# A fused attention and MLP kernel: the masks as second transfer, new planner constants and ranks

## The chip, the cores and the metric

The kernel runs on one core of a Trainium2 chip. A core has five engines that run their own instruction streams, each in order: TensorE (PE, matrix products; its weight loads are shown apart as PEld), VectorE (DVE), ScalarE (ACT), GpSimd (POOL) and SyncE (SP), which here issues all transfers between the chip's memory (HBM) and the on-chip memory (SBUF). Products accumulate in a small second on-chip memory, PSUM. The metric is the time of one execution on the device in microseconds (us), as the median of several runs.

## What is computed

Attention with two kinds of local masks, followed by a two-layer network whose activation is a rational function:

```python
scores = scale * np.matmul(q, k.transpose(0, 1, 3, 2))      # 8 batches, 8 heads, 576 x 64
mask_plain = (rel >= 0) & (rel < 32)                        # heads 0 to 3
mask_dil = (rel >= 0) & (rel < 128) & (rel % 4 == 0)        # heads 4 to 7
scores = np.where(masks[None, :, :, :], scores, -1000000000.0)
attn = softmax(scores)
x = (attn @ v), as 4608 tokens x 512
h = x @ w_in                                                # 512 -> 2048
P = a[0] + a[1] * h + a[2] * h**2 + a[3] * h**3
Q = 1.0 + np.abs(b[0]) * np.abs(h) + np.abs(b[1]) * h**2
out = (P / (Q + 1e-06)) @ w_out                             # 2048 -> 512
```

The two weight matrices come as 64-bit floats; the kernel takes their 32-bit words apart and joins them to 32-bit floats.

## The kernel before

**Attention in units.** Each of the 8 batches is cut into 6 units (48 in all, numbered batch * 6 + unit). A unit loads one tile of queries and keys (`load_qk`, 448 KB) and one of values (`load_v`, 384 KB). In the first two batches PE writes the masks into PSUM with a product by an identity and adds the scores to it (`scores`, lines 274 to 285), so a unit's scores need its qk and the masks `mask_t`, a 96 KB tile that is loaded once (line 903). Then follow the row maximum (`mx`, DVE), its subtraction, the exponential (ACT), the sum and reciprocal (DVE), the normalization (POOL), transposes (PE) with a copy (`pT`), and the product with the values (`av`). For the six units of batch 0 ACT evacuates the result to the high part of the MLP's input (`evac_hi`, tile `xh`) and DVE takes the low part (`xl`); each value is kept as a sum of two parts, for products at full precision. Batches from 2 on add the masks on DVE and turn their tiles by transposes on DVE and transfers.

**The MLP in tiles.** 9 chunks of 512 tokens times 16 slices of the hidden layer make 144 tiles, in an order given by `runs` and `tiles` (lines 963 and 964). A tile is 12 matmuls of PE into `h`, a chain on ACT, DVE and POOL (absolute value, the two linear parts, a logarithm and an exponential for the division, the products), and 12 matmuls `out` for four output banks. The first tiles need their slice of the weights: `plan_weights` (line 689) loads a 512 KB block (`wi0` to `wi15`, `wo0` to `wo15`), takes the words apart on ACT and POOL, joins them on DVE and splits the result in a high and a low part.

**The order is planned.** Nothing is issued directly. Each step is an `Op` with the engines that could run it, a cost in ns for each, a rank, its dependencies (`deps`), ops that must only be issued before it (`follows`) and buffers that it takes. `Plan.run` (line 128) simulates the engines at build time: again and again it takes the engine that can start first, picks the op of lowest rank among those that can start within 200 ns, and emits its instructions. What it emits is pinned, so each engine's instructions stand in the planner's order on the chip, and an instruction that waits holds back all that stand behind it on its engine. Transfers are planned as one pipe: the first is not through before `DMA_START`, each adds its bytes over `DMA_RATE`, and `DMA_NS` passes from the end of its bytes to its use (lines 86 and 170 to 172).

**Ranks.** The ranks are in units of one tile's number. `Plan.due` (line 106) counts backward: an op with a slack gets the least rank of what needs it, less its own cost over `PERIOD`, less its slack. A unit is due (`by`) at `last - (5 - u) * step`, with a pair (last, step) for each batch in `DUE` (line 32). Tiles from the 37th on get their steps' ranks from `LATE` (line 34), slacks come from `SLACK` (line 35): `qk0` and `v0` for the loads of batch 0, `wi`, `wo`, `w` and `out` for the weights and the early tiles. All loads of batch 0 and of the weights are sorted by rank, and each follows the one before it (lines 980 to 982).

The masks (`masked`, rank -39.4) and the six coefficients a and b (`lc`, rank -39.5, planned with 60 ns on SP) are two transfers more; the masks follow the coefficients. `coefs` (line 910, rank -30) prepares the coefficients with one small instruction on DVE and one on ACT; the first tile of the MLP needs it.

Of the kernel before, what the change touches and what calls it, by code (L numbers as in the profile page):

```python
# [28 lines left out]
START_S, START_O = ["A", "att"] * 3, ["B", "B", "B", "A", "B", "A"]  # L29
KIND = [0, 0, 0, 0, 1, 0] + [2] * 6  # L30
LESS = [0, 0, 0, 0, 1, 1]
DUE = [(-41.16, 11.47), (-146.25, 19.43), (423.68, 72.57), (61.95, 5.87), (470.95, -17.55), (494.47, -17.25), (93.76, -24.29), (711.56, 21.96)]

LATE = {"ab": -187.16, "ql": -342.11, "pl": -25.5, "qq": -118.36, "t1": -2.55, "t2": -120.77, "ln": 177.41, "ex": -496.7, "g0": -73.65, "g1": -54.63, "g2": -312.0, "gh": -189.38, "gl": 379.92, "out": 3.83}
SLACK = {"sc": 2.49, "qk0": -51.8, "v0": -50.12, "load": 7.26, "wi": 11.43, "wo": -2.45, "w": -16.22, "gl": -5.19, "out": -6.13}

EARLY_TILES, BOTH_TILES = 36, 36

# [40 lines left out]
class Plan:  # L79
# [3 lines left out]
    HOP = {"PE": 200.0, "ACT": 135.0, "DVE": 120.0, "POOL": 80.0, "SP": 0.0}  # L83
    MORE = {("PE", "ACT"): 40.0, ("ACT", "POOL"): 110.0, ("DVE", "POOL"): 110.0, ("DVE", "ACT"): 60.0, ("ACT", "DVE"): 15.0}
    DUE_HOP, WINDOW = 150.0, 200.0
    DMA_START, DMA_NS, DMA_RATE = 3300.0, 1750.0, 375.0
    PERIOD, PE_LATE = 4743.0, 105.0

    def __init__(self):
# [2 lines left out]
    def op(self, engs, rank, fn, *deps, dma=0, lock=False):  # L92
        o = Op(engs, rank, fn, deps, dma, lock)
        self.ops.append(o)
        return o
# [88 lines left out]
def tile_attention_moe(  # L184
# [21 lines left out]
    op = plan.op  # L206

    def load(dst, src):
        pin(nc.sync.dma_start(dst, src))  # L209
# [4 lines left out]
    def act(o, i, func, **kw):  # L214
        pin(nc.scalar.activation(o, i, func, **kw))  # L215

    def tt(o, x, y, op):
        pin(nc.vector.tensor_tensor(o, x, y, op))  # L218

    def stt(o, x, s, y, op0, op1):  # L220
        pin(nc.vector.scalar_tensor_tensor(o, x, s, y, op0, op1))  # L221
# [7 lines left out]
    def either(eng, o, x, y, alu):  # L229
        (ptt if eng == "POOL" else tt)(o, x, y, alu)  # L230
# [26 lines left out]
    class Unit:  # L257
# [251 lines left out]
        def plan(self, by, tags):  # L509
# [59 lines left out]
            for o in (sc, ma, mx, su, ex, sm, rc, no, tr, *self.placed, *([sb] if kind == 2 else [])):  # L569
                o.slack = 0.0  # L570
            sc.slack = SLACK["sc"]
            lq.slack = SLACK["qk0" if start else "load"]
            lv.slack = SLACK["v0" if start else "load"]
            plan.takes(lq, qt, 1 if start else LOADS, [sc])
# [67 lines left out]
    early, first_loads, unit_loads, left_done = [], [], [], []  # L642
# [46 lines left out]
    def plan_weights(key):  # L689
        f = op({"SP": 430}, 0, lambda e: w_fetch(key), dma=512 * (8 if wide else 4) * P)  # L690
        early.append(f)
        if len(joined) >= AHEAD:
            f.follows.append(joined[-AHEAD])
        if wide:
            sc = op({"ACT": 600}, 0, lambda e: w_scale(key), f)
            lw = op({"ACT": 690, "POOL": 690}, 0, lambda e: w_low(key, e), f, consts)
            jn = op({"DVE": 680}, 0, lambda e: w_join(key), sc, lw, lock=True)
            steps = [sc, lw, jn]
        else:
            steps = [op({"DVE": 335}, 0, lambda e: w_copy(key), f)]  # L700
        hi = op({"ACT": 550, "DVE": 460, "POOL": 620}, 0, lambda e: w_hi(key, e), steps[-1], lock=True)
        lo = op({"DVE": 602, "POOL": 1280}, 0, lambda e: w_lo(key, e), hi, lock=True)
        plan.takes(steps[0], "stage", STAGE, [lo])
        plan.takes(f, "%s%d" % key, 1, [steps[-1]])
        plan.takes(hi, "%s%d" % key, 1, [lo])
        joined.append(steps[-1])
        w_done[key] = lo
        for o in steps + [hi]:
            o.slack = 0.0
        lo.slack = SLACK[key[0]]  # L710
        f.slack = SLACK["w"]

# [10 lines left out]
    class Tile:  # L723
# [51 lines left out]
        def plan(self):  # L775
# [5 lines left out]
            Tile.last_h = h  # L781
            ab = op({"ACT": 480}, k + LATE["ab"], lambda e: self.abs(), h)
            ql = op({"ACT": 710}, k + LATE["ql"], lambda e: self.q_lin(), ab)
            pl = op({"ACT": 664}, k + LATE["pl"], lambda e: self.p_lin(), h)
            if tail:
                pl.follows.append(ql)
            qq = op(both, k + LATE["qq"], lambda e: either(e, self.a, self.r, self.a, ALU.mult), ql, lock=True)
            t1 = op({"DVE": 602}, k + LATE["t1"], lambda e: tt(self.t, self.t, self.ps, ALU.mult), pl, ab)
            t2 = op({"DVE": 663}, k + LATE["t2"], lambda e: stt(self.ps, self.t, na_t[:, 1:2], self.ps, ALU.add, ALU.mult), t1)
            ln = op({"ACT": 615}, k + LATE["ln"], lambda e: act(self.r, self.a, AF.Ln, bias=ln_bias, scale=2.0**-LOG_SHIFT), qq)  # L790
# [7 lines left out]
            if self.early:  # L798
                for o in (ab, ql, pl, qq, t1, t2, ln, ex, g0, g1, g2, gh):
                    o.slack = 0.0  # L800
                gl.slack = SLACK["gl"]
            outs = []
# [81 lines left out]
    coef_t = const.tile([P, 6], F32, name="coef_t")  # L884
# [3 lines left out]
    def make_coefs():  # L888
        pin(nc.vector.tensor_scalar(na_t, coef_t[:, 0:4], -1.0, None, ALU.mult))
        act(ab_t, coef_t[:, 4:6], AF.Abs)  # L890
# [7 lines left out]
    def memsets():  # L898
        pin(nc.gpsimd.memset(low_bias, LOW_BIAS))
        pin(nc.gpsimd.memset(ln_bias, GUARD * 2.0**-LOG_SHIFT))  # L900
        pin(nc.gpsimd.memset(exp_bias, -LOG_SHIFT * 0.6931471805599453))

    masked = op({"SP": 430}, -39.4, lambda e: load(mask_t, mask), dma=P * 768)
# [1 line left out]
    minus, less_ops = [], []  # L905
    plan.takes(identity, "gl", 2, less_ops)
    consts = op({"POOL": 80}, -87, lambda e: memsets())
    lc = op({"SP": 60}, -39.5, lambda e: load(coef_t, coef), dma=3000)
    masked.follows.append(lc)
    coefs = op({"DVE": 80}, -30, lambda e: make_coefs(), lc, consts)  # L910


# [1 line left out]
    for u in range(NU):  # L914
        tags = ((wpool, f"wi{15 - u}"), (wpool, f"wo{15 - u}"))
        last, step = DUE[0]
        Unit(0, u).plan(last - (NU - 1 - u) * step, tags)
    for key in keys:
        plan_weights(key)
    for b in range(1, B):  # L920
        last, step = DUE[b]
        for u in range(NU):
# [124 lines left out]
```

## Time and profile before

| | |
|---|---|
| median of 3 runs | 917.04 us (916.18 to 917.08) |
| the profiled execution | 916.49 us, of which the span from the first to the last instruction is 914.7 us |
| busy in the span | PE 883.2 us (97%), PEld 716.1, DVE 742.3 (81%), ACT 675.4 (74%), POOL 467.7 (51%) |
| instructions | 21129, of these 8153 matmuls |
| transfers | 103.46 MB, mean 113 GB/s |
| chain that ended last | PE 75%, DVE 11%, DMA 5%, ACT 5%, issue 3% |

The times in the profile run from the start of the span. A row of the timeline gives start, length, engine, line, operation, the written and the read tiles, and in brackets the idle time before it with what ended that. The row of a transfer on SPq is its issue; it lands later. The windows give busy times of each engine within a stretch, the granted clock of PE and the share and rate of the transfers. Where several instructions of one kind follow each other they are merged, with x and their count.

### The profile page before, as it was taken

The numbers are of one execution on the slowest core, as the hardware profiler recorded it, in microseconds if no ns is written. First come the engines' busy times: TensorE is split into PE (matmuls) and PEld (weight loads), VectorE is DVE, ScalarE is ACT, GpSimd is POOL, SyncE is SP. The second block draws the span as 40 slices with busy tenths as digits, with TensorE's granted clock in tenths as the row PEclk, the third lists the DMA queues.
The fourth block names the chain that finished last, engine by engine and source line by source line (L and its number), as shares of the span: only waits on it lengthen the run. The fifth ranks groups of instructions, "written<-read, shape, count | busy, mean of one in ns | idle before, by whom it ended". The sixth has DMA issues, their size and how long they took to land.

```text
span 914.7 us, 21129 instructions
## 1 busy us (share of the span) xinstructions
PE 883.2 (97%) x8153; PEld 716.1 (78%) x8153; DVE 742.3 (81%) x1312; ACT 675.4 (74%) x1092; POOL 467.7 (51%) x408
## 2 busy tenths in 40 slices
PE   5877999999999999999999999999999999999998
PEld 3755787887877878888888888888888788888876
DVE  4789999999988988788978888887779677566656
ACT  2676888877666777877787778677777688778764
POOL 2454554656635554555455555546455545444442
PEclk9989999999999999999999999999999999999999
DMA  9667460235633343334334324423333220001001
GB/s 359 240 221 249 154 234 1 99 124 190 198 99 110 110 134 118 119 111 125 115 113 127 121 83 146 129 82 85 115 95 91 61 69 1 1 1 47 0 1 47
DMA packets 85477, 103.46 MB, mean 113 GB/s; under 512 B 37376, under 2 KB 62848, under 8 KB 85376
## 3 DMA queue, kind: packets, MB, share of 16 engines
q1 hardware_dynamic: 85376, 102.11, 34.5%
q8 instruction: 64, 1.05, 0.5%
q14 instruction: 37, 0.30, 0.1%
HBM read 75.21 MB, written 26.87 MB: 112 GB/s over the span
## 4 chain that ended last, share of the span: by engine, by line
PE 75%; DVE 11%; DMA 5%; ACT 5%; issue 3%; POOL 1%; SPq 1%; DVEq 0%; POOLq 0%; ACTq 0%
PE out L212 34%; PE h L212 34%; PE pair L212 5%; DVE h L221 3%; DVE a L221 2%; DMA wi_raw<-in_w_in_dram 2%; ACT r L215 2%; DVE t L218 1%; DVE a L218 1%; DVE gl L218 1%; DMA wo_raw<-in_w_out_dram 1%; SPq L209 1%; DMA qk<-in_qk_dram 1%; ACT a L215 1%; PE pair_B L212 1%
## 5 line engine op out<-in xcount | busy, mean ns | idle before, releaser
L212 PE MATMUL h<-xh,wi 128*128 128x512 f32 x1136 | 378.1, 394 | 6.8 <-DVE a L221 6.5
L212 PE MATMUL out<-gh,wo 128*128 128x512 f32 x1136 | 353.8, 393 | 0.7 <-DVE os L218 0.7
L224 POOL TENSOR_TENSOR a<-r,a 128x512 f32<-128x512 f32 x121 | 156.6, 1294 | 241.1 <-ACT r L215 233.4
L212 PEld LDWEIGHTS h<-xh,wi 128*128 128x128 f32 x1136 | 214.5, 189 | 58.3 <-DVE a L221 12.6
L212 PEld LDWEIGHTS out<-gh,wo 128*128 128x128 f32 x1136 | 211.2, 188 | 45.9 <-DVE os L218 1.1
L212 PE MATMUL out<-gl,wo 128*128 128x512 f32 x568 | 221.8, 391 | 1.6 <-DVE gl L218 1.0
L212 PE MATMUL h<-xl,wi 128*128 128x512 f32 x568 | 222.4, 391 | 0.0
L224 POOL TENSOR_TENSOR gl<-a,gh 128x512 fp32r<-128x512 f32 x129 | 175.1, 1357 | 64.7 <-ACT gh L215 64.0
L221 DVE SCALAR_TENSOR_TENSOR h<-h,na_t,r 128x512 f32<-128x512 f32 x142 | 106.9, 753 | 111.0 <-ACT r L215 109.2
L215 ACT ACTIVATE r<-a,ln_bias 128x512 f32<-128x512 f32 x141 | 101.9, 723 | 82.8 <-POOL a L224 80.3
L215 ACT ACTIVATE r<-a,ab_t 128x512 f32<-128x512 f32 x141 | 114.7, 814 | 16.3 <-DVE a L221 14.5
L212 PEld LDWEIGHTS out<-gl,wo 128*128 128x128 f32 x568 | 106.6, 188 | 25.6 <-POOL gl L224 1.5
L212 PEld LDWEIGHTS h<-xl,wi 128*128 128x128 f32 x568 | 107.3, 189 | 21.5
L215 ACT ACTIVATE a<-h 128x512 f32<-128x512 f32 x140 | 83.5, 596 | 53.7 <-PE h L212 35.0
L215 ACT ACTIVATE t<-h,na_t 128x512 f32<-128x512 f32 x142 | 109.6, 772 | 5.0 <-PE h L212 4.6
L221 DVE SCALAR_TENSOR_TENSOR h<-t,na_t,h 128x512 f32<-128x512 f32 x142 | 107.3, 756 | 4.9
L215 ACT ACTIVATE r<-r,exp_bias 128x512 f32<-128x512 f32 x144 | 104.3, 724 | 4.7
L218 DVE TENSOR_TENSOR t<-t,h 128x512 f32<-128x512 f32 x142 | 96.6, 681 | 7.2 <-ACT t L215 7.1
L221 DVE SCALAR_TENSOR_TENSOR a<-a,r 128x512 f32<-128x512 f32 x141 | 100.2, 711 | 0.0
L221 DVE SCALAR_TENSOR_TENSOR a<-a,h 128x512 f32<-128x512 f32 x140 | 96.2, 687 | 4.8
L215 ACT ACTIVATE gh<-a 128x512 fp32r<-128x512 f32 x130 | 81.5, 627 | 23.2 <-PE out L212 14.9
L224 POOL TENSOR_TENSOR p<-p,sm 128x384 f32<-128x384 f32 x48 | 47.7, 993 | 34.3 <-DVE sm L352 28.1
(115 smaller groups left out, 712.4 us busy)
## 6 DMA issues: line engine op xcount, KB each, us to landing
qk<-in_qk_dram SPq DMA_DIRECT2D x48, 448.0 KB, 5.0
v<-in_vp_dram SPq DMA_DIRECT2D x48, 384.0 KB, 3.7
out_dram<-os SPq DMA_DIRECT2D x36, 256.0 KB, 2.3
wi_raw<-in_w_in_dram SPq DMA_DIRECT2D x16, 512.0 KB, 6.1
wo_raw<-in_w_out_dram SPq DMA_DIRECT2D x16, 512.0 KB, 6.9
results<-y SPq DMA_DIRECT2D x42, 192.0 KB, 2.4
z<-results SPq DMA_DIRECT2D x168, 48.0 KB, 2.5
turned<-u SPq DMA_DIRECT2D x36, 192.0 KB, 2.0
```

The source lines that it names most:

```text
L209: pin(nc.sync.dma_start(dst, src))
L212: pin(nc.tensor.matmul(o, lhs, rhs, start=start, stop=stop, skip_group_check=free))
L215: pin(nc.scalar.activation(o, i, func, **kw))
L218: pin(nc.vector.tensor_tensor(o, x, y, op))
L221: pin(nc.vector.scalar_tensor_tensor(o, x, s, y, op0, op1))
L224: pin(nc.gpsimd.tensor_tensor(o, x, y, op))
```

## The change

The masks' transfer now follows the first unit's load of queries and keys (`first_loads[0]`), and the coefficients and the next two loads of batch 0 (`first_loads[1:3]`: the first unit's values and the second unit's queries and keys) follow the masks. The coefficients' transfer is planned with 430 ns on SP instead of 60 and rank -39.3. The planner's constants for transfers are other ones, and so are all pairs of `DUE`, all `LATE` and all `SLACK` values.

```diff
-DUE = [(-41.16, 11.47), (-146.25, 19.43), (423.68, 72.57), (61.95, 5.87), (470.95, -17.55), (494.47, -17.25), (93.76, -24.29), (711.56, 21.96)]
-LATE = {"ab": -187.16, "ql": -342.11, "pl": -25.5, "qq": -118.36, "t1": -2.55, "t2": -120.77, "ln": 177.41, "ex": -496.7, "g0": -73.65, "g1": -54.63, "g2": -312.0, "gh": -189.38, "gl": 379.92, "out": 3.83}
-SLACK = {"sc": 2.49, "qk0": -51.8, "v0": -50.12, "load": 7.26, "wi": 11.43, "wo": -2.45, "w": -16.22, "gl": -5.19, "out": -6.13}
+DUE = [(-38.22, 22.7), (-174.68, 8.39), (477.36, 65.7), (58.21, 6.13), (336.77, -13.09), (465.22, -18.48), (177.99, -28.14), (667.75, 10.86)]
+LATE = {"ab": -277.93, "ql": -318.77, "pl": 80.35, "qq": -46.56, "t1": 3.11, "t2": -68.73, "ln": 311.13, "ex": -566.86, "g0": -69.06, "g1": -64.01, "g2": -259.86, "gh": -249.94, "gl": 474.78, "out": 3.38}
+SLACK = {"sc": 1.09, "qk0": -48.46, "v0": -47.6, "load": -17.12, "wi": 8.03, "wo": -2.51, "w": -16.13, "gl": -8.5, "out": -9.65}
...
-    DMA_START, DMA_NS, DMA_RATE = 3300.0, 1750.0, 375.0
+    DMA_START, DMA_NS, DMA_RATE = 1000.0, 1700.0, 380.0
...
-    lc = op({"SP": 60}, -39.5, lambda e: load(coef_t, coef), dma=3000)
-    masked.follows.append(lc)
+    lc = op({"SP": 430}, -39.3, lambda e: load(coef_t, coef), dma=3000)
     coefs = op({"DVE": 80}, -30, lambda e: make_coefs(), lc, consts)
...
         Unit(0, u).plan(last - (NU - 1 - u) * step, tags)
+    masked.follows.append(first_loads[0])
+    for o in (lc, *first_loads[1:3]):
+        o.follows.append(masked)
     for key in keys:
         plan_weights(key)
```

## The prediction

> **What bounds the kernel now.** I read the sums of page 1 and the windows by stage first, to see where TensorE (PE) is not busy; then the waits of PE; then the timeline of the first 20 us. The stages (core 0: us of the stretch, then busy us and instructions of PE, PEld, DVE, ACT, POOL, clock, DMA share, GB/s):
> ```profile
> 0.00:100.00 100.00, 76.29 (x1467) 59.80 (x1468) 76.82 (x160) 60.54 (x124) 41.46 (x55) 0.95 0.71 250
> 100.00:300.00 200.00, 196.66 (x1754) 157.16 (x1753) 187.50 (x323) 155.61 (x250) 108.73 (x95) 1.00 0.43 139
> 300.00:875.00 575.00, 574.55 (x4780) 470.25 (x4779) 454.28 (x797) 436.37 (x686) 303.92 (x249) 1.00 0.28 86
> 875.00:915.00 40.00, 35.66 (x156) 28.86 (x155) 23.72 (x35) 22.83 (x34) 13.54 (x11) 1.00 0.07 27
> ```
> PE idles 23.7 us of the first 100, 3.3 of the next 200, 0.5 of the next 575 and about 4 in the tail. From 100 us on the kernel is PE-bound, so what the change is worth is decided in the fill: each us by which PE gets its work earlier there moves everything behind it. The first line of PE's waits shows how the fill begins (total us, times, longest):
> ```profile
> PE pair_A L212 <- DMA mask_t<-in_mask_dram: 7.3, 1, 7.3
> ```
> The longest single wait is for the masks. The timeline of the transfer queue and of PE (start, length):
> ```profile
> 0.72 0.38 SPq L209 DMA_DIRECT2D qk<-in_qk_dram  x1
> 1.16 0.42 SPq L209 DMA_DIRECT2D v<-in_vp_dram  x1
> 1.63 0.42 SPq L209 DMA_DIRECT2D qk<-in_qk_dram  x1
> 2.10 0.43 SPq L209 DMA_DIRECT2D coef_t<-in_coef_dram  x1
> 2.57 0.43 SPq L209 DMA_DIRECT2D mask_t<-in_mask_dram  x1
> ...
> 7.31 0.48 PE L212 MATMUL pair_A<-mask_t,ident_b 128*128 128x192 bf16 x2 [7.31 <-DMA mask_t<-in_mask_dram]
> ...
> 9.05 0.97 PE L212 MATMUL pair<-qk 64*32 64x64 f32 x48
> ...
> 10.38 0.97 PE L212 MATMUL pair_A<-qk 64*32 64x64 f32 x48
> ...
> 12.39 0.97 PE L212 MATMUL pair<-qk 64*32 64x64 f32 x48
> ```
> Unit 0 needs only its own queries and keys and the masks, but the masks are fifth in the queue. PE starts at 7.31; units 1, 2 and 3 multiply from 9.05, 10.38 and 12.39.
>
> **The masks, second.** After the change the queue's order is fixed by the new follows-edges and the ranks. Rank of a qk load = its unit's due time, minus the planner's chain behind it (13.3 us of costs over the 4743 ns period: 2.8), minus the slacks. With the new numbers the loads of units 0 to 5 get about -107.2, -84.5, -61.8, -39.1, -16.4 and 6.3 (before: -52.0 to 5.3). So: qk0, masks, v0, qk1, v1, qk2, v2, then the coefficients (rank -39.3, just ahead of qk3), qk3, and so on. How much data had moved by when, and two landings:
> ```profile
> 0.00:3.50 3.50, 0.00 (x0) 0.10 (x1) 0.00 (x0) 1.28 (x1) 1.71 (x12) 1.00 0.49 165
> 0.00:6.20 6.20, 0.00 (x0) 0.10 (x1) 0.00 (x0) 1.28 (x1) 1.71 (x12) 1.00 0.70 229
> 0.00:8.30 8.30, 0.99 (x45) 0.79 (x50) 0.17 (x1) 1.49 (x2) 1.71 (x12) 1.00 0.78 274
> 0.00:10.40 10.40, 3.09 (x105) 1.95 (x105) 1.63 (x4) 1.98 (x3) 1.71 (x12) 1.00 0.84 302
> DMA to landing us min/median/max: 4.7/4.7/4.7
> DMA to landing us min/median/max: 3.1/5.8/11.0
> ```
> The first four rows are windows (the last number is GB/s), the other two are the answers by tile, the masks' and the qk's. Moved: 0.58 MB by 3.5 us, 1.42 by 6.2, 2.27 by 8.3, 3.14 by 10.4. A qk is 0.459 MB, a v 0.393, the masks 0.098. Masks and all before them are 1.41 MB, moved by 6.2; they were used at 7.31, so a transfer is usable about 1.1 us after its bytes' turn. Now:
> - masks: qk0 plus masks are 0.56 MB, turn at 3.4, usable at about 4.6 in place of 7.31: **2.7 us** earlier. Bounds: issue at 1.16 plus the shortest qk landing 3.1 gives 4.3; plus the masks' own 4.7 gives 5.9.
> - unit 1: 1.41 MB, so 7.3 where it multiplied at 9.05: 1.75 earlier. Its qk lands 0.3 to 0.4 later than before; that is hidden, as PE took it up only at 9.05.
> - unit 2: 2.26 MB, 9.4 against 10.38: 1.0 earlier. Unit 3: 3.12 MB, 11.5 against 12.39: 0.9 earlier.
>
> From unit 4 on I take the loads to run ahead of PE: a qk and a v, 0.85 MB, take 2.1 us at 0.41 MB per us (0.87 MB from 8.3 to 10.4), and PE reaches the first h, with the sixth unit behind it, only at 41.89 (row below). So of 2.7 us at the head the supply of data leaves between 0.9 (units 2 and 3) and 2.7 (unit 0's own softmax, which now runs before the others crowd VectorE). I take the middle, **1.8 us**.
>
> **The weights step behind.** Ranks of the weights' loads are also new: the first w_in goes from 3.4 to 6.7, which puts it behind the sixth qk (6.3); the first w_out goes from 11.1 to 7.6. Before, the first w_in is waited for on ScalarE, ahead of unit 0's evacuation:
> ```profile
> 15.36 1.67 PE L212 MATMUL pair_B<-pT,v 64*64 64x32 f32 x48
> 17.24 0.78 ACT L215 ACTIVATE wi_raw<-wi_raw,low_bias 128x512 int32<-128x512 uint32 x1 [1.37 <-DMA wi_raw<-in_w_in_dram]
> 17.92 0.64 ACT L663 ACTIVATE wi_f<-wi_raw 128x512 f32<-128x512 f32 x1
> 18.47 0.47 ACT L215 ACTIVATE xh<-pair_B 128x384 fp32r<-128x384 f32 x1
> ...
> 20.91 0.76 ACT L215 ACTIVATE wi_raw<-wi_raw,low_bias 128x512 int32<-128x512 uint32 x1 [1.00 <-DMA wi_raw<-in_w_in_dram]
> ...
> 41.89 0.50 PE L212 MATMUL h<-xh,wi 128*128 128x512 f32 x1
> ```
> The product is complete at 17.03, but ScalarE, which runs in order, sits on the weights until 17.24 and evacuates at 18.47: 1.4 us lost on the way of unit 0, whose buffer pair_B the next unit needs. By the planner's own lines (86 and 170 to 172) this was meant: with its old first time (3300 ns) the masks land at 8.8 and the first w_in at 18.1 of its clock, 9.3 apart, while unit 0 needed 17.03 - 7.31 = 9.7. With the new constants and order the masks land at 4.2 and the first w_in at 17.5 (1000 + 5.34 MB at 380 B per ns + 1700 ns), 13.3 apart. Unit 0 is then ready 3.6 us ahead, and goes first on ScalarE. I take the whole **1.4 us**; bounds 0 (another wait stands there) and 2.4 (the next such wait, 1.0 us at 20.91, goes too). The weights come 1.1 us later (one qk more at 0.4 MB per us); their cover is that the first h matmul starts only at 41.89. If that cover is gone, it costs the 1.1.
>
> **Coefficients.** They move from fourth to eighth; by the sum above they land near 10.4 (2.66 MB), where they were used before the masks came at 7.31. Their two small instructions on VectorE and ScalarE have rank -30, behind all the early units, and the planner believes in a landing at 9.7 of its clock, so they stand behind unit 0's reductions; nothing but the first MoE tile needs them. Cost taken: 0; bounds 0 and 1.7 (second rival). The planner's 430 for 60 ns is a cost, no instruction.
>
> **The other ranks.** From 300 to 875 us there are 0.5 us of idle PE to win, so new LATE and DUE values there can only cost; the planner keeps PE fed now, and I take 0, with a loss up to the size of the 3.3 idle of 100 to 300. In the fill, 40 to 110 us, they deal the cards anew. What is at stake there, in rows of PE's timeline and, with the clock as the third number from the end, of the windows:
> ```profile
> 48.34 0.72 PE L212 MATMUL pair<-v,pT 64*32 64x64 f32 x48 [2.46 <-ACT p L215]
> 51.69 1.65 PE L212 MATMUL pair<-mx,ident 128*128 128x192 f32 x4 [1.46 <-DVE mx L312]
> 49.30:56.10 6.80, 5.34 (x62) 4.40 (x62) 6.42 (x13) 5.77 (x11) 3.08 (x4) 0.50 0.69 212
> 89.19 0.50 PE L212 MATMUL h<-xh,wi 128*128 128x512 f32 x1 [3.35 <-DVE a L221]
> 90.30:93.70 3.40, 3.40 (x10) 2.66 (x9) 3.37 (x6) 3.05 (x6) 2.17 (x2) 0.50 0.03 7
> 110.32 0.50 PE L212 MATMUL h<-xh,wi 128*128 128x512 f32 x1 [1.21 <-DVE a L221]
> 61.71 0.75 PE L212 MATMUL out<-gh,wo 128*128 128x512 f32 x2
> 40.00:110.00 70.00, 58.29 (x785) 44.96 (x784) 63.01 (x119) 51.81 (x90) 33.57 (x33) 0.93 0.65 223
> ```
> Gaps of 2.46 us (to 48.34) and 3.35 us (to 89.19) are each followed by a stretch at half clock, 6.8 us long (a gap of 1.46 lies inside it) and 3.4 us long, which cost up to half of that: 3.4 and 1.7 us. A gap of 1.21 us is followed by none. A new order can lose these stretches (gain up to 5.1) or make another (loss 1.7 beside its gap). Nothing in the profile says which; I take 0.
>
> The Trainium skill, "TensorE: Matmul & The Clock Gate", section "HAM oscillation — how this bites in real kernels", states that gaps up to about 3.4 us leave the clock alone. This trace does not agree: the first drop follows a gap of 2.46. By the rule only a longer gap than any here would do it and the slower rival below would cost 3.35 without its 1.7; by the rows it costs both.
>
> **The sum.** 1.8 + 1.4 = 3.2 us. The profiled execution took 916.49 us, span 914.70 with 1.79 around it; 916.49 - 3.2 = 913.3. The median of the runs, 917.04, lies 0.55 above that execution, so I predict 913.8.
>
> **Rivals.**
> - *The supply of data binds anyway.* Units 2 and 3 gain only 0.9, and where ScalarE still waits for the first w_in, which lands 1.1 us later, that is given back. For it: from 3.5 to 10.4 us 2.57 MB came, 0.37 MB per us, without a pause. Against it: PE took until 41.89 to reach the first h, so that 20 us of other work lie between. 916.49 - 0.9 + 1.1 + 0.55 = 917.2, chance 0.16.
> - *The wait for the coefficients takes the masks' place.* If VectorE meets them ahead of unit 0's maximum, that starts at 10.5, where the masks and the scores let it start at 7.31 + 0.48 + 0.97 = 8.8: 1.7 later. 916.49 + 1.7 + 0.55 = 918.7, chance 0.04.
> - *A new gap in the fill (slower).* VectorE is busy 63 of the 70 us from 40 to 110, and PE waits for its last instruction of a tile (the 3.35 at 89.19). If the new order puts one more weight join or attention step ahead of such an instruction, PE idles once more for about 3.35 and then runs at half clock for 3.4 us. It decides once a gap passes 1.2 (no drop) towards 2.5 us (drop). With the head's 1.8 kept: 916.49 - 1.8 + 3.35 + 1.7 + 0.55 = 920.3, chance 0.20.
> - *One or both half-clock stretches vanish.* Earlier w_out may help: the first out matmul starts only at 61.71, and with its weights there sooner it could fill a gap such as the 1.46 us. 913.8 - 3.4 = 910.4, both 908.7; chance 0.15.
>
> **How the numbers follow.** The forecast has 0.45. A difference of 0.2%, 1.8 us, is about what a measurement of this kernel can tell from no change. Faster: the forecast and the last rival, 0.60, less 0.02 for forecasts that end above 915.2: 0.58. Slower: the gap with 0.20 and half of the second rival: 0.22. The rest, 0.20, is within it. The range goes from 909.0 (both stretches gone) to 920.5 (a gap).
>
> **What would show it.** Right: the first PE matmul at about 4.6 us, units 1 to 3 at about 7.3, 9.4 and 11.5; no wait of ScalarE for w_in ahead of unit 0's evacuation, which comes at about 14 to 16 instead of 18.47; the PE-bound stretch as before, 3 us earlier. Wrong: the first matmul past 5.9; the first h matmul not before 41; a third half-clock stretch between 36 and 110 us, or new idle PE past 300 us.

## The result

The kernel after the change takes 925.0 us (median of 4 runs, 922.58 to 925.93); the kernel before, run beside it, 916.61 (914.95 to 917.08). The ratio is 1.0095, 95% interval 1.0077 to 1.0113: slower by 8.7 us, where 913.8 was predicted and 920.5 was the upper end. The profiled execution of after took 922.58 us with a span of 920.8, 6.1 longer than before's 914.7; it is the shortest of the four, so the profile shows 6.1 of the 8.7 us.

**The windows by stage**, with the same limits as before (us of the stretch, then busy us and instructions of PE, PEld, DVE, ACT, POOL, clock, DMA share, GB/s), and the stretch from 100 to 200 by itself:
```profile
0.00:100.00 100.00, 78.47 (x1471) 61.15 (x1471) 75.42 (x157) 64.16 (x131) 49.41 (x58) 0.93 0.80 273
100.00:300.00 200.00, 193.52 (x1639) 154.05 (x1640) 185.32 (x315) 151.90 (x245) 102.09 (x92) 0.99 0.39 125
300.00:875.00 575.00, 574.20 (x4863) 468.20 (x4862) 448.85 (x789) 431.98 (x674) 305.93 (x264) 1.00 0.28 87
...
100.00:200.00 100.00, 93.56 (x661) 72.91 (x661) 94.39 (x146) 78.87 (x127) 54.98 (x47) 0.98 0.33 110
```
Up to 100 us PE idles 2.2 us less than before (21.5 against 23.7), from 100 to 300 it idles 3.1 more (6.5 against 3.3): 4.95 more from 100 to 200 (6.44 against 1.49) and 1.8 less behind it. From 300 us on it is bound by PE as before. So the idle time that is new lies between 100 and 200 us. PE is also busy for longer, and the clock's column hints at a part of that. The stretches at half clock in after:
```profile
49.40:56.20 6.80, 5.17 (x107) 4.19 (x108) 5.57 (x13) 4.28 (x8) 1.40 (x2) 0.50 0.66 216
63.00:69.80 6.80, 5.75 (x106) 4.56 (x107) 5.65 (x12) 4.65 (x9) 3.34 (x3) 0.50 0.81 259
124.50:127.90 3.40, 3.40 (x9) 2.63 (x8) 3.37 (x6) 2.25 (x5) 1.78 (x2) 0.50 1.01 338
```
Before had 10.2 us of half clock with 8.74 of PE's work in them; after has 17.0 with 14.32. If that work took twice its time, half of the 5.58 more, 2.8 us, is lost by it. The sums of page 1 in after:
```profile
PE 887.9 (96%) x8153; PEld 717.3 (78%) x8153; DVE 737.3 (80%) x1300; ACT 675.1 (73%) x1086; POOL 474.0 (51%) x426
```
PE is busy for 4.7 us more than before (883.2) and idle for 1.4 more (32.9 of 920.8 against 31.5 of 914.7): the 6.1. Of the 4.7 the half clock would account for 2.8; no view places the other 1.9. But the half clock doesn't tell a slow kernel from a fast one here: e1 below, which is no slower than before, has 17.0 us of it in its profile too (from 27.7, 48.2 and 89.1 us), and over the 71 executions of before that were timed beside the runs the mean granted clock goes from 0.981 to 0.996, with a median of 916.1 us for the 23 lowest and 915.6 for the 21 highest. What it costs after isn't shown.

**The waits of PE** (total us, times, longest) name who keeps it waiting:
```profile
PE h L212 <- DVE a L221: 7.2, 8, 2.4
PE pair_A L212 <- DMA mask_t<-in_mask_dram: 4.3, 1, 4.3
PE pair L212 <- DVE mx L312: 3.7, 3, 1.9
PE out L212 <- POOL gl L224: 2.9, 3, 1.6
...
PE pair L212 <- DMA qk<-in_qk_dram: 2.1, 1, 2.1
```
The masks' wait fell from 7.3 to 4.3. A wait for queries and keys of 2.1 us is new. The first row is hardly more than before's 6.5 in all, but from 100 to 200 us alone it reads, before and after:
```profile
PE h L212 <- DVE a L221: 1.2, 1, 1.2
PE h L212 <- DVE a L221: 4.4, 4, 2.4
```
One wait for DVE's last instruction of a tile has become four there. **The timeline of the head** of after:
```profile
0.72 0.38 SPq L209 DMA_DIRECT2D qk<-in_qk_dram  x1
1.16 0.42 SPq L209 DMA_DIRECT2D mask_t<-in_mask_dram  x1
...
4.33 0.48 PE L212 MATMUL pair_A<-mask_t,ident_b 128*128 128x192 bf16 x2 [4.33 <-DMA mask_t<-in_mask_dram]
...
8.24 0.97 PE L212 MATMUL pair<-qk 64*32 64x64 f32 x48 [2.11 <-DMA qk<-in_qk_dram]
10.36 0.97 PE L212 MATMUL pair_A<-qk 64*32 64x64 f32 x48 [0.71 <-DMA qk<-in_qk_dram]
...
11.50 0.17 DVE L889 TENSOR_SCALAR na_t<-coef_t 128x4 f32<-128x4 f32 x1 [1.10 <-DMA coef_t<-in_coef_dram]
...
16.11 0.49 ACT L215 ACTIVATE xh<-pair_B 128x384 fp32r<-128x384 f32 x1 [0.93 <-PE pair_B L212]
...
19.32 0.74 ACT L215 ACTIVATE wi_raw<-wi_raw,low_bias 128x512 int32<-128x512 uint32 x1 [1.11 <-DMA wi_raw<-in_w_in_dram]
```
PE starts 3.0 us earlier. Unit 1 gains only 0.8 (8.24 for 9.05), unit 2 nothing (10.36 for 10.38). Unit 0's evacuation comes at 16.11 for 18.47, and the wait for the first w_in now stands behind it. The first h matmul comes at 40.60, 1.3 us earlier than before's 41.89. So the head gained a part of what it should, and the time went elsewhere.

**Where it went** shows in the timeline from 119 us on:
```profile
119.16 1.30 POOL L224 TENSOR_TENSOR wo<-wo_f,wo 128x512 fp32r<-128x512 f32 x1
...
119.93 0.76 DVE L221 SCALAR_TENSOR_TENSOR h<-t,na_t,h 128x512 f32<-128x512 f32 x1
...
120.41 1.27 POOL L224 TENSOR_TENSOR wi<-wi_f,wi 128x512 fp32r<-128x512 f32 x1
120.59 1.64 DVE L221 SCALAR_TENSOR_TENSOR a<-a,r 128x512 f32<-128x512 f32 x1
122.27 0.69 DVE L221 SCALAR_TENSOR_TENSOR a<-a,h 128x512 f32<-128x512 f32 x1
...
123.01 0.50 PE L212 MATMUL h<-xh,wi 128*128 128x512 f32 x1 [2.42 <-DVE a L221]
```
PE waits 2.42 us for DVE's last read of the tile's `h`; 1.5 us later the clock halves. What made DVE late here is one instruction of its own: `a<-a,r` takes 1.64 us. It began while POOL made the low part of a weight block (`w_lo`, a subtraction of two tiles), and it ended at 122.23, 0.55 after POOL's end at 121.68. The group of that instruction from 100 to 200 us (count, busy us, mean ns), before:
```profile
L221 DVE SCALAR_TENSOR_TENSOR h<-t,na_t,h 128x512 f32<-128x512 f32 x17 | 12.8, 755 | 0.5
...
L221 DVE SCALAR_TENSOR_TENSOR a<-a,r 128x512 f32<-128x512 f32 x17 | 12.6, 743 | 0.0
```
and after:
```profile
L221 DVE SCALAR_TENSOR_TENSOR a<-a,r 128x512 f32<-128x512 f32 x16 | 13.9, 866 | 0.0
...
L221 DVE SCALAR_TENSOR_TENSOR h<-t,na_t,h 128x512 f32<-128x512 f32 x15 | 11.3, 755 | 0.5
```
`a<-a,r` grew from 743 to 866 ns; `h<-t,na_t,h`, of the same size, stayed at 755, even beside POOL at 119.93. The first reads two tiles of SBUF, the second has one operand in PSUM. From 100 to 200 us such subtractions hold four `a<-a,r` in after, at 112.73, 120.59, 170.61 and 177.82, for 0.59 to 0.96 us each beyond the usual 0.68; in before they hold one, at 120.16, for 0.66. The Trainium skill, "SBUF — State Buffer", section "SBUF: two separate sides", says that DVE and POOL share a pair of ports under an exclusive lock, which the one that starts first keeps for its whole instruction, and that a DVE instruction with two SBUF inputs fully blocks against a POOL instruction that reads SBUF. These rows agree: DVE began 0.18 us behind POOL and ended 0.55 behind its end.

The planner knows such a port: `Plan.shares` (line 103) counts every step on POOL, and every step on DVE that is marked with `lock`, and lets no two of them run at once. `a<-a,r` is so marked, and the subtraction runs on POOL, so in the plan the two never meet. On the chip they do; there the order of each engine is the plan's, but the times are its own.

### The profile page after: what moved, and what is told of

Read it like the earlier page. It is cut to its first block, busy times and chain, and to the rows that moved or that the text cites. A ratio compares the mean times of both kernels' runs of the same rounds, so it can differ in the third digit from the quotient of the medians.

```text
span 920.8 us, 21164 instructions
## 1 busy us (share of the span) xinstructions
PE 887.9 (96%) x8153; PEld 717.3 (78%) x8153; DVE 737.3 (80%) x1300; ACT 675.1 (73%) x1086; POOL 474.0 (51%) x426
## 3 DMA queue, kind: packets, MB, share of 16 engines
q8 instruction: 64, 1.05, 0.5%
## 4 chain that ended last, share of the span: by engine, by line
PE 77%; DVE 9%; ACT 3%; issue 2%; DMA 1%; POOL 1%; SPq 0%; DVEq 0%; ACTq 0%; POOLq 0%
PE h L212 37%; PE out L212 36%; PE pair L212 5%; DVE a L221 3%; DVE h L221 2%; ACT r L215 1%; DMA z<-results 1%; DVE t L218 1%; DVE a L218 1%; DVE wi_f L221 1%; DVE gl L218 0%; POOL a L224 0%; ACT a L215 0%; DVE wo_f L221 0%; ACT xh L215 0%
## 5 line engine op out<-in xcount | busy, mean ns | idle before, releaser
L224 POOL TENSOR_TENSOR a<-r,a 128x512 f32<-128x512 f32 x124 | 160.4, 1294 | 280.8 <-ACT r L215 263.1
L224 POOL TENSOR_TENSOR gl<-a,gh 128x512 fp32r<-128x512 f32 x130 | 170.6, 1312 | 37.4 <-ACT gh L215 30.3
L221 DVE SCALAR_TENSOR_TENSOR a<-a,r 128x512 f32<-128x512 f32 x141 | 105.8, 750 | 0.0
L215 ACT ACTIVATE gh<-a 128x512 fp32r<-128x512 f32 x136 | 85.1, 626 | 27.3 <-PE out L212 18.7
L224 POOL TENSOR_TENSOR p<-p,sm 128x384 f32<-128x384 f32 x48 | 43.1, 899 | 36.1 <-DVE sm L352 30.0
```

Source lines behind the costliest of these rows:

```text
L224: pin(nc.gpsimd.tensor_tensor(o, x, y, op))
```

## The experiments

**Theory P**: the head's gain is real but small, and the new order loses more than that in the fill, because POOL's weight splits now fall beside DVE's last instructions of a tile. **Rivals**: the loss comes from the head (transfers, coefficients); from the new transfer constants; or from gaps around 60 us with the half clock behind them. All ratios are to the kernel before on the same chip.

| run | edit | median, us | ratio, 95% |
|---|---|---|---|
| e1 | before, masks issued second | 915.15 | 0.9988 (0.9978 to 0.9997) |
| e5 | e1, and unit 0's evacuation ahead of w_in | 914.98 | 0.9987 (0.9975 to 1.0000) |
| e12 | e1, and coefficients' instructions later | 914.69 | 0.9981 (0.9971 to 0.9992) |
| e2 | after, masks issued fifth | 925.05 | 1.0093 (1.0072 to 1.0114) |
| e3 | after, coefficients issued fifth | 923.9 | 1.0083 (1.0068 to 1.0098) |
| e7 | before and the new edges, planned again | 942.14 | 1.0272 (1.0252 to 1.0292) |
| e4 | e7 and the new transfer constants | 945.29 | 1.0321 (1.0298 to 1.0344) |
| e8 | after, old transfer constants | 928.02 | 1.0124 (1.0107 to 1.0142) |
| e6 | after, POOL's low part as one copy | 917.63 | 1.0016 (1.0005 to 1.0027) |
| e9 | before, POOL's low part as one copy | 915.72 | 0.9993 (0.9982 to 1.0004) |
| e10 | after, that copy made twice | 921.7 | 1.0058 (1.0043 to 1.0073) |
| e11 | after, all low parts on DVE | 925.71 | 1.0103 (1.0090 to 1.0116) |
| e13 | after, one copy for the late blocks | 918.81 | 1.0029 (1.0012 to 1.0046) |
| e14 | after, one copy for the early blocks | 922.04 | 1.0065 (1.0039 to 1.0091) |

### The head: e1, e2, e3, e5, e12

These keep the order of every engine's instructions and move only what is named. In e1 the plan is that of before, but the masks' transfer is issued behind unit 0's queries and keys:
```diff
+            if self.n == 0:
+                load(mask_t, mask)
...
-    masked = op({"SP": 430}, -39.4, lambda e: load(mask_t, mask), dma=P * 768)
+    masked = op({"SP": 430}, -39.4, lambda e: None, dma=P * 768)
```


> The order of before on every engine is kept, and only the masks' transfer is issued second. Theory 1 (the new ranks' order in the fill loses the time, the masks themselves are harmless): first matmul at 4.3 us, units 1 to 3 at about 8.2, 10.4 and 12.5 as in after, ScalarE still waits for the first w_in at 17.2, so most of the 3 us are lost there: 0 to 1.5 us faster than before. Theory 2 (the masks' small transfer ahead delays the second qk by more than it gives): 2 us slower or more.

e2 is the mirror: after's order, with coefficients and masks issued fourth and fifth again; e3 moves the coefficients alone, behind unit 1's queries and keys.

> The order of after on every engine is kept, and only the first transfers are issued as in before: qk0, v0, qk1, coefficients, masks. Theory 1: within 2 us of after (925), slower if at all, since the first matmul goes back to 7.3 us. Theory 2: 3 us faster than after or more, as the second qk lands at 6.9 again.

> The order of after on every engine is kept, and only the coefficients are issued right behind the second qk, fifth instead of eighth. Theory 1: the wait of VectorE and ScalarE for them at 10.4 to 11.5 us goes, the end moves by 0 to 1.1 us. Theory 3 (that wait starts the loss): 3 us faster than after or more.

In before's order the masks' place is worth 1.1 us (0.3 to 2.0 by the interval), in after's nothing (1.0093 against 1.0095), and the coefficients' place can't be told from nothing. So the head doesn't carry the loss. The first windows of after, in which the kernel before moved 165, 229 and 302 GB/s:
```profile
0.00:3.50 3.50, 0.00 (x0) 0.10 (x1) 0.00 (x0) 1.28 (x1) 1.70 (x12) 1.00 0.47 148
0.00:6.20 6.20, 1.81 (x52) 1.07 (x52) 0.46 (x1) 1.28 (x1) 1.70 (x12) 1.00 0.66 190
...
0.00:10.40 10.40, 3.26 (x109) 1.98 (x112) 3.13 (x7) 1.80 (x2) 2.53 (x13) 1.00 0.80 270
```
and of e2, where only the masks' and the coefficients' places differ:
```profile
0.00:6.20 6.20, 0.00 (x0) 0.10 (x1) 0.00 (x0) 1.28 (x1) 1.70 (x12) 1.00 0.68 223
```
By 6.2 us 1.18 MB had moved in after and 1.38 in e2. In this pair the pipe moves 0.2 MB less with the masks second, twice the masks' own 0.098. The 13 profiles with the masks second have 1.12 to 1.33 MB by then, the three with the masks fifth 1.38 to 1.42. Why, no run shows.

e5 is e1 with ScalarE's two instructions on the first w_in held back behind unit 0's evacuation:
```diff
+            while self.n == 3 and held:
+                held.pop(0)()
...
+        if key == ("wi", 0) and not late:
+            held.append(lambda: w_scale(key, True))
+            return
...
```


> The kernel of the first experiment (order of before, masks second), and on ScalarE the two instructions on the first w_in moved behind unit 0's evacuation and unit 3's exponential; nothing else moves. Theory A (the prediction's second term): unit 0 is evacuated at about 16.4 us instead of 18.9, unit 1's product with the values starts at about 17.6 instead of 20.0, and 1.0 to 1.4 us arrive at the end: 913.8 to 914.2. Theory B (that time is absorbed before the first h matmul, which something else sets): 0 to 0.4 us at the end.

It is the prediction's second term by itself, and it can't be told from nothing (0.9987 against 0.9988, each with about 1 us to either side). ScalarE's timeline in e5 shows what takes it up:
```profile
16.45 0.49 ACT L215 ACTIVATE xh<-pair_B 128x384 fp32r<-128x384 f32 x1 [0.65 <-PE pair_B L212]
...
21.20 0.77 ACT L215 ACTIVATE wi_raw<-wi_raw,low_bias 128x512 int32<-128x512 uint32 x1 [1.64 <-DMA wi_raw<-in_w_in_dram]
21.87 0.47 ACT L215 ACTIVATE xh<-pair_B 128x384 fp32r<-128x384 f32 x1
```
Unit 0 goes early, at 16.45, but unit 1's evacuation at 21.87 again stands behind a w_in, the next one; in e1 it came at 22.03. The first h matmul starts at 39.56, in e1 at 39.72. In e1 DVE met the coefficients ahead of unit 0's maximum, as the prediction's second rival had it:
```profile
8.25 0.17 DVE L891 TENSOR_SCALAR na_t<-coef_t 128x4 f32<-128x4 f32 x1 [8.25 <-DMA coef_t<-in_coef_dram]
8.32 0.55 DVE L314 TENSOR_REDUCE mx<-pair_A 128x6 f32<-128x384 f32 x1
```
e12 is e1 with those two instructions behind unit 1's subtraction.

> The first experiment (order of before, masks second) with the two instructions on the coefficients moved behind unit 1's subtraction, so that unit 0's maximum does not wait for their landing at 8.25 us. If the head counts (theory H): unit 0's maximum at 5.6 instead of 8.3, and 0.5 to 1.5 us at the end, 913.5 to 914.7. If units 2 and 3 are bound by their data at 10.2 and 12.3 anyway (theory D): within 0.4 us of 915.1.

The maximum then starts at 5.63, 2.7 earlier, and the time isn't told apart from e1, nor theory H from theory D. e12 is the fastest kernel here: 0.19% under the kernel before, 0.08 to 0.29% by its interval.

### The plan: e7, e4, e8

> Before with the masks second and the coefficients' edges and cost of the change, planned anew with the old constants and the old ranks. If the ranks hold beyond the plan they were found for (theory R): within 2 us of the first experiment, 913 to 917. If a new plan from unfitted ranks is a lottery (theory 4): anywhere, up to the 945 of the run with the old ranks.

> After with the old DUE, LATE and SLACK: masks second and the new constants for transfers stay, and the order is planned anew from the old ranks. Theory 1: the w_in come before the w_out again, no PE-idle of 5 us between 100 and 200 us; 915 to 919. Theories 2 and 3: still 922 or more. Theory 4 (any new plan is a lottery of some us, whatever its ranks): anything from 912 to 926.

> After with the old constants for transfers (3300, 1750, 375) and everything else of the change, planned anew. Theory R: within 3 us of after, 922 to 928. Theory 4: anywhere from 914 to 945.

e7 has before's ranks and constants and only the new edges (with the coefficients' cost and rank), e4 the new constants too, e8 is after with the old ones. Planned again with ranks that were found for another order, the kernel takes 942 and 945 us; e4's 945 is outside every range that was set for it. From 200 to 300 us e7 shows
```profile
200.00:300.00 100.00, 84.11 (x963) 65.74 (x962) 81.05 (x154) 55.70 (x92) 34.49 (x35) 0.91 0.48 149
```
15.9 us of idle PE, where after has nearly none. So the new ranks repair most of what the new edges break in the plan (25 us in e7, 29 in e4) and leave 8.7. Going back to the old constants doesn't help: with them after is 3 us slower.

### POOL beside DVE: e6, e9, e10, e11, e13, e14

e6 takes the suspect out of after: POOL makes the low part as one copy (0.62 us, one operand) in place of the subtraction (1.28, two). The kernel leaves the subtraction out there, so its output is another one; the same holds for e9, e10, e13 and e14.
```diff
     def w_lo(key, eng):
+        if eng == "POOL":
+            copy(eng, wt[key][:, 1], wf.pop(key))
+            return
```


> After, with the low part of those weight blocks that GpSimd splits taken as a plain copy of the block (one operand, about 0.6 us) instead of the subtraction of the high part (two operands, 1.28 us); the output is changed by it. Theory P (GpSimd's two-operand instructions stretch VectorE's instructions on the path of the tiles): the stretched VectorE instructions between 100 and 200 us lose 2 us or more, PE idles 4.5 us or less there instead of 6.6, and the end comes 2 to 5 us earlier. Theory Q (VectorE is late there by the order of its own instructions): within 1 us of after.

> The control of the run with the plain copy: the same edit in before (GpSimd takes the low part of its weight blocks as one copy; the output is changed by it). Before gives GpSimd as many of these as after does, 22 and 23 of 32. Theory P (in after, GpSimd's two-operand instructions fall on VectorE's path, in before they mostly don't): at most 2 us faster than before. Theory S (GpSimd's shorter work is worth 7 us in any of these kernels, and after's loss is another one): 5 us faster or more.

It gives back 7.2 us of the 8.7 (1.0016 against 1.0095, of 916.6), more than the 2 to 5 that theory P had, while the same edit in before (e9) gives 0.6 and its interval holds 1. So it isn't that POOL has less to do as such: in after's order the split stands where it hurts. e10 makes the copy twice, which fills POOL's time again with one operand at a time, and e11 moves all splits to DVE.

> After with that copy made twice, one behind the other: GpSimd is busy as long as with the subtraction (2 x 0.62 against 1.28 us), but with one-operand instructions; the output is changed by it. Theory P1 (the two operands hold VectorE up): as fast as with one copy, 916 to 919. Theory P2 (GpSimd's time counts, since what comes behind on GpSimd is late): 922 to 926, as after.

> After with every low part of the weights subtracted on VectorE, at the planned place; 23 move there, 0.68 us each, 16 us in all. Theory P1: the stretched instructions between 100 and 200 us shrink, but VectorE has 94.4 us of work in these 100 and takes on some 9: PE idles more there than it gains, 925 to 932. Theory P2: GpSimd's load was what delayed, and it is gone: 916 to 921.

e10 lies half-way, 3.4 us under after and 3.9 over e6, in the range of neither theory. The number of operands isn't what holds DVE, for in e10 a copy held `a<-a,r` as well, until 0.54 us after its end:
```profile
122.16 0.61 POOL L236 TENSOR_SCALAR wi<-wi_f 128x512 fp32r<-128x512 f32 x1
122.30 1.01 DVE L221 SCALAR_TENSOR_TENSOR a<-a,r 128x512 f32<-128x512 f32 x1
```
A shorter instruction on POOL holds DVE for less. A copy also differs from the subtraction in that it need not wait for the high part. How the 7.2 us divide between the holding, POOL's time and that wait, these runs don't separate. e11 gains nothing, by theory P1 because DVE must then do what POOL no longer does: PE idles 9.6 us from 100 to 200 in it. e13 and e14 have the single copy for the blocks of slices 6 and up (from about 90 us on) and for slices 0 to 5.
```diff
+        if eng == "POOL" and key[1] >= 6:
```


> The kernel after, where GpSimd makes the weights' low part as one copy (0.6 us, one operand) only for the blocks of slices 6 and up, that is from about 90 us on; the earlier ones stay a subtraction of 1.28 us. The low part of those blocks is then the whole value, so the output is another. If the loss comes from VectorE's instructions held between 100 and 200 us (theory), nearly all of the 7.4 us that the copy everywhere gave comes back: 917 to 919 us, and VectorE's stretch of 100 to 200 us falls from 6.5 towards 3.6. If it comes from the early blocks, through the gaps around 60 us ahead of the second stretch at half clock (rival), 922 to 925.

> The mirror of the run before: the copy only for the blocks of slices 0 to 5, up to about 70 us; the later ones stay a subtraction. By the theory that the loss is made between 100 and 200 us: 922 to 925 us. By the rival that the gaps around 60 us and the half clock behind them carry it: 920 or less, with no half clock at 63 us. If each half gives some 3 to 4 us, both run at about 921.

The late blocks give 6.0 us back (1.0029), the early ones 2.8 (1.0065, with an interval that overlaps that of after). The theory had 917 to 919 and 922 to 925; both hold, the second only just. In e13 the place of the 2.42 us wait reads
```profile
118.62 0.62 POOL L236 TENSOR_SCALAR wi<-wi_f 128x512 fp32r<-128x512 f32 x1
...
119.45 0.68 DVE L221 SCALAR_TENSOR_TENSOR a<-a,r 128x512 f32<-128x512 f32 x1
120.17 0.69 DVE L221 SCALAR_TENSOR_TENSOR a<-a,h 128x512 f32<-128x512 f32 x1
...
120.91 0.50 PE L212 MATMUL h<-xh,wi 128*128 128x512 f32 x1 [1.47 <-DVE a L221]
```
`a<-a,r` is back at 0.68, 0.96 shorter, and PE's wait is 0.95 shorter; no half clock follows it. The group of that instruction from 100 to 200 us is back at 680 ns:
```profile
L221 DVE SCALAR_TENSOR_TENSOR a<-a,r 128x512 f32<-128x512 f32 x17 | 11.6, 680 | 0.0
```
The stretch from 100 to 200 us of e13:
```profile
100.00:200.00 100.00, 95.60 (x683) 76.19 (x683) 96.29 (x158) 80.59 (x130) 48.72 (x49) 1.00 0.33 109
```
PE idles 4.4 us in it: 2.0 less than in after, still 2.9 more than in before (row below). That rest of 2.9 comes from something other than these late subtractions; no run says what.
```profile
100.00:200.00 100.00, 98.51 (x696) 78.61 (x695) 97.34 (x155) 83.97 (x135) 57.39 (x47) 1.00 0.36 122
```
One thing in e13 isn't its edit's: its second half-clock stretch, at 67 us ahead of the first copy, is 3.4 us long where after's is 6.8. Executions differ in this by themselves: e13's runs go from 915.4 to 921.15, so the interval counts here, not the one profile.

## Why the prediction was wrong

- **The masks, second: the mechanism was right, and its size isn't refuted in the old order.** The queue's order was as worked out, and the first matmul came at 4.33 (4.6 predicted, 4.3 the bound). Units 1 to 3 were put at 7.3, 9.4 and 11.5 and came at 8.24, 10.36 and 12.53, since the sum took the bytes to flow as before. For the 1.8 us that it took, the runs have 1.1 (0.3 to 2.0) in e1 and 1.7 (0.7 to 2.7) in e12, where the coefficients stand behind as the prediction had them. In after's order the same place is worth nothing that shows (e2).
- **The weights step behind: right in what moved, wrong in what it is worth.** The evacuation came at 16.11 with w_in's wait behind it. "I take the whole" 1.4 us was the upper choice: e5 measures 0.1, the lower bound that stood beside it (another wait stands there), with 1.4 at the edge of what the intervals leave. The working has a slip, too: 1000 + 5.34 MB at 380 + 1700 is 16.8, not 17.5, so the masks and the first w_in are 12.6 apart and unit 0 is 2.9 us ahead; the order on ScalarE came out the same.
- **Coefficients: cost 0 isn't refuted.** e3 can't be told from after.
- **The other ranks: here the prediction failed.** It put the whole new order at nothing: for the fill, "Nothing in the profile says which; I take 0", and behind it, "the planner keeps PE fed now, and I take 0, with a loss up to the size of the 3.3 idle of 100 to 300". The new order costs 9.8 us beside e1 (1.0095 less 0.9988), and 7.2 of the 8.7 us over before go when POOL's subtractions become copies (e6). The four plans tried here (after, e8, e7, e4) lie 9 to 29 us above the kernel before. A new plan can make idle time that the old one has not, so the idle time of before bounds nothing. The signs of being wrong missed the place as well: they watched 36 to 110 us and from 300 on, where nothing of the kind came, and the waits came between 110 and 200.
- **The slower rival was near, with another cause, a later place and under half the size.** It said that PE would wait for DVE's last instruction of a tile in the fill, and run at half clock behind it. That is the 2.42 us at 123.01 and the stretch from 124.5. It put this down to one more join or attention step in DVE's order; the runs show POOL's subtraction holding one DVE instruction instead. It allowed for one more such gap; from 100 to 200 us there were three more (four for one), and e14 suggests that the early subtractions cost something too. The half clock that it priced at 1.7 us doesn't set after apart from e1.
- **Its bound on the clock** ("It decides once a gap passes 1.2 (no drop) towards 2.5 us (drop)") went by the length of a single gap, and that alone doesn't decide. After's stretch from 63.0 us begins in the second of two gaps that are each far below 2.5:
```profile
60.47 0.72 PE L212 MATMUL pair<-v,pT 64*32 64x64 f32 x48 [1.39 <-DVE y L413]
...
63.30 1.65 PE L212 MATMUL pair<-mx,ident 128*128 128x192 f32 x4 [1.18 <-DVE mx L312]
```
and in e14 a gap as long as after's was followed by none:
```profile
121.52 0.50 PE L212 MATMUL h<-xh,wi 128*128 128x512 f32 x1 [2.41 <-DVE a L221]
```

What stays open: why the pipe is slower with the masks second; the 1.5 us that after keeps over before without POOL's subtractions, and 2.9 us of idle PE from 100 to 200; how the 7.2 us divide; and why more subtractions meet `a<-a,r` on the chip in the new order, when the plan keeps the two apart in either. How far the chip's times are from the plan's at these places, no run shows.

## What to carry to other kernels

When ranks or costs of a planned order change, the local edit is the small part: freeze the order and move the one transfer to price it (here -1.1 us), and treat the new order as a draw whose spread is known only from other plans (here 9 to 29 us worse). Where an engine's last instruction of a tile sets the next tile's start, look at which instructions of the other engines run beside it: here an instruction that reads two SBUF tiles on DVE was held until POOL's was through, though the planner keeps the two apart by its own clock. An early wait that is removed is worth only what the next wait of the same kind leaves.

## What was not expected of the hardware

- A DVE instruction of 0.68 us with two SBUF operands ended 0.55 us after POOL's subtraction that it met, both at 120.59 in after and in e14 at the same place (POOL to 120.20, DVE to 120.75):
```profile
118.94 1.26 POOL L224 TENSOR_TENSOR wi<-wi_f,wi 128x512 fp32r<-128x512 f32 x1
119.12 1.63 DVE L221 SCALAR_TENSOR_TENSOR a<-a,r 128x512 f32<-128x512 f32 x1
```
It is held until POOL is through, not slowed in proportion, whatever POOL is at: in the 16 profiles 215 `a<-a,r` take over 0.8 us, all of them began while POOL was at an instruction (products and subtractions, in four cases instructions with one operand), 0.02 to 1.05 us behind its start, and all ended 0.53 to 0.55 us after its end.
- Two waits of 1.39 and 1.18 us, 2.8 us apart, went with 6.8 us at half clock, while a single one of 2.41 was followed by none.
- With a 96 KB transfer in second instead of fifth place 0.05 to 0.3 MB less had moved by 6.2 us.
- Two profiles with 17.0 us at half clock, e1 and after, lie 7.3 us of span apart, and before with 10.2 us lies 1.2 above e1.
